# Output tiles copied from PSUM by ScalarE, the last one in halves, and transposes placed between output pieces in the last stretch

## Chip, cores and metric

One core of one Trainium2 chip. The metric is the device time of one execution in microseconds, the median of several runs. A trace is one profiled execution; times in it count from the start of its span, which is some 1.8 us shorter than the device time of that run (359.7 against 361.45). The experiments ran on several chips (8, 14, 11 and 12 in the record); a ratio compares runs of one occasion only, and the granted TensorE clock was 0.998 to 1.0 of full speed in every run for which it is listed.

## The reference

Two layers in a row. Clustered attention: each query and key is assigned to the nearest of 16 centroids of its head, and a query sees only keys of its own cluster. Then a gated feed-forward layer with RMS normalisation on the 3072 x 512 result.

```python
scores = where(q_assign == k_assign, q @ k.T / 8, -1e9)      # 4 batches, 8 heads, 768 x 64
x = softmax(scores) @ v                                      # becomes 3072 x 512
xn = x / sqrt(mean(x * x) + 1e-6) * rms_g
g = xn @ w_gate                                              # 512 x 1536
out = (g * sigmoid(g) * (xn @ w_val)) @ w_out                # 1536 x 512, float32
```

## The kernel before

The work is cut into eight units of 384 rows. While TensorE does the attention of unit u, the feed-forward products of units u-1 and u-2 are placed between its score products as filling. At a border between two stretches the normalised x of one unit is transposed, and the three output tiles of the unit before it are finished. Seven such borders exist: six lie beside attention, the last one has only feed-forward work around it.

TensorE's products go to tiles in PSUM, which the kernel takes in banks. All of `tq`, `tx`, gate, value and output products share three PSUM banks that rotate; a new tile waits until the one that had its bank has been read out (0.25 us listed for an output tile at 134.36 us, 0.77 us for the third transposes of the last border, both shown in the prediction).

```python
ps_s = pool("ps_s", 2, space=PSUM)      # scores, two banks each
ps_a = pool("ps_a", 1, space=PSUM)
ps_g = pool("ps_g", 3, space=PSUM)      # the three rotating banks
...
def rms(u):                             # sums of squares on ScalarE, the rest on VectorE
    ...
    for t in range(nt):
        squares(u, t, True)
    ...
def xtrans(u, c):
    ...
    ps = ps_g.tile([P, UQ], BF16, tag="gen", name="tx")
    ...
    for t in range(UNITS[u][2]):
        nc.tensor.transpose(ps[:, t * P:(t + 1) * P], xn[u][:, t, c * P:(c + 1) * P], ident)
    nc.vector.tensor_scalar_mul(xnT[u][:, c, :w], ps[:, :w], gcol[:, c:c + 1])
...
def out_mm(u, t, part):                 # an output tile, in three parts of four products
    ...
    if part == 0:
        outs[u] = ps_g.tile([P, DM], F32, tag="gen", name="o")
    for f in range(4 * part, 4 * part + 4):
        nc.tensor.matmul(outs[u], lhsT=gvT[u][:, f, t * P:(t + 1) * P], rhs=wo[:, f], start=f == 0, stop=f == FC - 1)
    if part == 2:
        o = outp.tile([P, DM], F32, tag="o_sb", name="o_sb")
        nc.vector.tensor_copy(o, outs[u])
        ...
        nc.sync.dma_start(out=rows[...], in_=o)
...
        # o: the nine output pieces of a border; ffn[:4]: its four transposes of x
        fill += o[:-3] + ffn[:2] + o[-3:-2] + ffn[2:3] + o[-2:-1] + ffn[3:4] + o[-1:] + spread(ffn[CC:CUT], prep)
        attention([(u, h) for h in range(H)], fill, 1)
...
rms(NU - 1)                             # the last border: outputs first, then the transposes
for _, f in out_work(NU - 2) + ffn_work(NU - 1) + out_work(NU - 1):
    f()
```

(Cuts are marked with dots; the comments are added here.)

The softmax here doesn't subtract the row's maximum and nothing guards it: scores larger than these inputs give would overflow.

## Time and profile before

| | before |
|---|---|
| time, median of 3 runs | 361.62 us (361.56 to 361.79) |
| span in the trace | 359.7 us |
| TensorE / ScalarE / VectorE busy | 96% / 71% / 66% |
| one output copy on VectorE, 128 x 512 | 0.69 us, 24 times |
| one table load on ScalarE (ACT_TABLE_LOAD) | 1.28 us, 3 times (at 2.63, 4.15 and 323.55 us) |
| TensorE's listed waits for output copies | 1.4 us, 5 times |

The first three rows say where to look: with TensorE at 96%, only its gaps can be won, and the last row lists those that belong to output copies. The lines themselves are in the prediction. In lines of the profile PE is TensorE (PEld its weight loads), DVE VectorE, ACT ScalarE, POOL GpSimd and SP SyncE; a q behind the name marks an instruction that only issues a transfer, and L379 is a line of that run's kernel. A timeline line gives the start, the duration, what ran and how often; the brackets hold the engine's idle time before it and what ended that. Lines of timelines are picked, those between are left out.

### The profile page before, as it was taken

Reading aid. Unit: us, or ns where it says so; the run is one execution under the profiler, and the core shown is the slowest. Engines: PE = TensorE matmul, PEld = TensorE weight load, DVE = VectorE, ACT = ScalarE, POOL = GpSimd, SP = SyncE. Lnnn points to the kernel's source line nnn. Section 1 sums busy time; section 2 is a strip of 40 time slices with the busy share of each in tenths; the row PEclk is TensorE's granted clock in tenths of the full one; section 3 lists DMA queues with packets and bytes.
Section 4 is the critical chain, followed back from the end, with each engine's and each line's share of the span. In section 5 each row is a group of like instructions: output and inputs, shape, how many; then the busy total and the mean of one; then the engine's idle time right before and its main releaser. Section 6 shows DMA issues by size and latency. Waiting matters only on the chain.

```text
span 359.7 us, 8049 instructions
## 1 busy us (share of the span) xinstructions
PE 345.2 (96%) x3027; PEld 210.0 (58%) x3047; DVE 237.1 (66%) x577; ACT 256.1 (71%) x455; POOL 110.2 (31%) x221
## 2 busy tenths in 40 slices
PE   8999799999999999999999999999999999999995
PEld 4555455655575656755576556756566656654552
DVE  5994379596567874686667865687656575677332
ACT  5789977996588866887588865978668866861320
POOL 1699306896051801535033711327000000000000
PEclk9999999999999999999999999999999999999999
DMA  7549999962154102610130002001010001002002
GB/s 256 185 121 212 244 241 270 334 190 67 64 157 133 24 29 89 202 40 19 59 118 2 16 8 87 2 2 24 38 52 3 0 31 58 2 3 80 8 2 87
DMA packets 28039, 32.03 MB, mean 89 GB/s; under 512 B 4960, under 2 KB 24928, under 8 KB 28000
## 3 DMA queue, kind: packets, MB, share of 16 engines
q1 hardware_dynamic: 18352, 24.75, 21.6%
q0 software_dynamic: 9072, 5.98, 10.0%
q10 hardware_dynamic: 576, 0.79, 0.7%
q8 instruction: 24, 0.39, 0.4%
q14 instruction: 15, 0.12, 0.1%
HBM read 28.35 MB, written 6.29 MB: 96 GB/s over the span
## 4 chain that ended last, share of the span: by engine, by line
PE 71%; DVE 14%; ACT 8%; issue 3%; POOL 1%; DMA 1%; SPq 0%; DVEq 0%; ACTq 0%
PE gate L357 16%; PE val L357 16%; PE s L284 13%; PE o L379 12%; PE acc L302 8%; ACT pT L288 5%; PE tq L200 4%; DVE o_sb L382 2%; PE sc L255 2%; ACT xn L322 2%; DVE xn L334 1%; PE warm L112 1%; DVE th L366 1%; DVE kext L214 1%; DVE scT L258 1%
## 5 line engine op out<-in xcount | busy, mean ns | idle before, releaser
L288 ACT ACTIVATE pT<-s,off 128x768 bf16<-128x768 f32 x192 | 171.0, 902 | 50.2 <-PE s L284 49.1
L284 PE MATMUL s<-qext,kext 80*128 80x384 bf16 x384 | 93.5, 325 | 3.0 <-ACT pT L288 2.6
L357 PE MATMUL gate<-xnT,wg 128*128 128x384 bf16 x384 | 78.5, 325 | 0.2 <-DVE xnT L345 0.2
L357 PE MATMUL val<-xnT,wv 128*128 128x384 bf16 x384 | 78.1, 326 | 0.4 <-DVE th L366 0.3
L366 DVE SCALAR_TENSOR_TENSOR th<-th,gate 128x384 f32<-128x384 f32 x84 | 46.3, 552 | 44.0 <-ACT th L365 43.6
L379 PE MATMUL o<-wo,gvT 128*128 128x512 bf16 x272 | 68.8, 378 | 2.1 <-DVE o_sb L382 1.0
L206 POOL CAST qext<-qkT 64x384 bf16<-64x384 f32 x64 | 33.0, 524 | 93.7 <-ACT qkT L202 92.1
L284 PEld LDWEIGHTS <-kext 80*128 80x128 bf16 x384 | 37.0, 98 | 35.3 <-issue 7.7
L365 ACT ACTIVATE th<-gate 128x384 f32<-128x384 f32 x84 | 41.1, 489 | 15.8 <-PE gate L357 15.2
L357 PEld LDWEIGHTS <-wv 128*128 128x128 bf16 x384 | 36.1, 97 | 26.1 <-issue 4.5
L370 DVE SCALAR_TENSOR_TENSOR gvT<-th,val 128x384 bf16<-128x384 f32 x84 | 46.1, 548 | 7.4 <-PE val L357 2.3
L357 PEld LDWEIGHTS <-wg 128*128 128x128 bf16 x384 | 35.8, 97 | 24.5 <-issue 3.6
L302 PEld LDWEIGHTS <-pT 128*128 128x128 bf16 x1152 | 43.5, 97 | 9.3 <-ACT pT L288 0.6
L302 PE MATMUL acc<-vbf,pT 128*128 128x65 bf16 x1152 | 45.6, 193 | 0.5 <-ACT pT L288 0.5
L379 PEld LDWEIGHTS <-gvT 128*128 128x128 bf16 x288 | 27.0, 97 | 27.7 <-issue 2.0
L202 ACT COPY qkT<-tq 128x384 f32<-128x384 f32 x64 | 29.2, 488 | 5.9 <-PE tq L200 5.0
L200 PE MATMUL tq<-ident_f,qk 128*128 128x128 f32 x192 | 30.2, 280 | 1.6 <-ACT qkT L202 1.2
L268 POOL DMA_DIRECT2D qext<-oh x48 | 23.1, 490 | 24.5 <-DVE oh L246 24.3
L200 PEld LDWEIGHTS tq<-ident_f,qk 128*128 128x128 f32 x192 | 23.2, 143 | 8.7 <-ACT qkT L202 2.2
L214 DVE TENSOR_SCALAR kext<-qkT 64x384 bf16<-64x384 f32 x60 | 23.8, 396 | 2.3 <-ACT qkT L202 1.6
L382 DVE COPY o_sb<-o 128x512 f32<-128x512 f32 x24 | 16.4, 686 | 12.5 <-PE o L379 12.5
L268 POOL DMA_DIRECT2D kext<-oh x48 | 22.9, 485 | 2.4 <-DVE th L366 1.2
(63 smaller groups left out, 241.9 us busy)
## 6 DMA issues: line engine op xcount, KB each, us to landing
qk<-in_q_dram SPq DMA_DIRECT2D x32, 192.0 KB, 3.9
vs<-in_v_dram SPq DMA_DIRECT2D x32, 192.0 KB, 3.7
out_dram<-o_sb SPq DMA_DIRECT2D x24, 256.0 KB, 2.0
qk<-in_k_dram SPq DMA_DIRECT2D x28, 192.0 KB, 4.0
wg<-in_moe_w_gate_dram POOLq DMA_DIRECT2D x4, 384.0 KB, 12.4
wv<-in_moe_w_val_dram POOLq DMA_DIRECT2D x4, 384.0 KB, 14.8
wo<-in_moe_w_out_dram POOLq DMA_DIRECT2D x3, 512.0 KB, 24.7
kext<-oh POOLq DMA_DIRECT2D x52, 12.0 KB, 1.6
```

The lines of the kernel that those rows point to most:

```text
L200: nc.tensor.transpose(ps[:, i * P:(i + 1) * P], qk[:, part, 2 * i:2 * i + 2].rearrange("p t d -> p (t d)"), ident_f)
L202: nc.scalar.copy(qkT[g, h // 2][:, h % 2, part], ps)
L206: nc.gpsimd.tensor_copy(qext[g % 4][:D, h, e * UQ:(e + 1) * UQ], qkT[g, h // 2][e * D:(e + 1) * D, h % 2, 0])
L268: on.dma_start(out=ext[D:D + NC, h, e * UQ:(e + 1) * UQ], in_=oh[32 * h + e * NC:32 * h + (e + 1) * NC])
L284: nc.tensor.matmul(ps[:, j, :w] if nt == HT else flat[:, j * w:(j + 1) * w], lhsT=kext[g % 4][:KR, hh, kc * P:(kc + 1) * P], rhs=qext[g % ...
L288: nc.scalar.activation(pT[u, h][:, n * i:n * i + n, :w], of, ACT.Exp, bias=off, scale=scale * ZS)
L302: nc.tensor.matmul(acc[:, h % 2, t], lhsT=pT[u, h][:, kc, t * P:(t + 1) * P], rhs=vbf[g % 4][:, hh, kc % HT * 2 + kc // HT], start=kc == 0 ...
L357: nc.tensor.matmul(ps, lhsT=w[:, c, f * P:(f + 1) * P], rhs=xnT[u][:, c, :n], start=c == 0, stop=c == CC - 1)
L365: nc.scalar.activation(th, ps, ACT.Tanh, scale=0.5)
L366: nc.vector.scalar_tensor_tensor(th, th, 1.0, ps, op0=ALU.add, op1=ALU.mult)
L370: nc.vector.scalar_tensor_tensor(gvT[u][:, f, :n], gates[u], 0.5, ps, op0=ALU.mult, op1=ALU.mult)
L379: nc.tensor.matmul(outs[u], lhsT=gvT[u][:, f, t * P:(t + 1) * P], rhs=wo[:, f], start=f == 0, stop=f == FC - 1)
```

## The change

Its intent: take the output copies from VectorE, which at a border is busy with the normalisation (131.14 to 132.42 us in the border shown below), to ScalarE, which idles there (1.22 us before the exponential at 133.87); fill the wait of the last border by mixing transposes and output pieces as in the other borders; halve the last copy, on which the end of the kernel hangs.

```diff
         if part == 2:
             o = outp.tile([P, DM], F32, tag="o_sb", name="o_sb")
-            nc.vector.tensor_copy(o, outs[u])
-            ...
-            nc.sync.dma_start(out=rows[...], in_=o)
+            ...                          # rows, now with the row index in it
+            if (u, t) == (NU - 1, HT - 1):
+                c = DM // 2
+                nc.vector.tensor_copy(o[:, :c], outs[u][:, :c])
+                nc.sync.dma_start(out=rows[:, :c], in_=o[:, :c])
+                nc.scalar.copy(o[:, c:], outs[u][:, c:])
+                nc.scalar.dma_start(out=rows[:, c:], in_=o[:, c:])
+            else:
+                nc.scalar.copy(o, outs[u])
+                nc.sync.dma_start(out=rows, in_=o)
...
+    def border(o, ffn):
+        return o[:-3] + ffn[:2] + o[-3:-2] + ffn[2:3] + o[-2:-1] + ffn[3:4] + o[-1:]
...
-    for _, f in out_work(NU - 2) + ffn_work(NU - 1) + out_work(NU - 1):
+    for _, f in border(out_work(NU - 2), ffn_work(NU - 1)) + ffn_work(NU - 1)[CC:] + out_work(NU - 1):
         f()
```

More of the change, by code (lines that the diff above doesn't have):

```diff
@@ L381, in out_mm @@
             o = outp.tile([P, DM], F32, tag="o_sb", name="o_sb")
-            nc.vector.tensor_copy(o, outs[u])
-            rows = out[b * S:(b + 1) * S].rearrange("(p t) f -> p t f", t=ST)
-            nc.sync.dma_start(out=rows[:, (col + t) % HT * 2 + (col + t) // HT], in_=o)
+            rows = out[b * S:(b + 1) * S].rearrange("(p t) f -> p t f", t=ST)[:, (col + t) % HT * 2 + (col + t) // HT]
+            if (u, t) == (NU - 1, HT - 1):
[7 more added lines that the diff above has]
+                nc.sync.dma_start(out=rows, in_=o)
     def group_work(g):
@@ L571 @@
         fill += [(0.0, lambda u=u: rms(u - 1))] + head
-        fill += o[:-3] + ffn[:2] + o[-3:-2] + ffn[2:3] + o[-2:-1] + ffn[3:4] + o[-1:] + spread(ffn[CC:CUT], prep)
+        fill += border(o, ffn) + spread(ffn[CC:CUT], prep)
         attention([(u, h) for h in range(H)], fill, 1)
```

## The prediction

> **What bounds the kernel now.** I read the busy shares first, then the slices, then who waits for whom on TensorE, and last the timeline around those waits.
>
> ```profile
> PE 345.2 (96%) x3027; PEld 210.0 (58%) x3047; DVE 237.1 (66%) x577; ACT 256.1 (71%) x455; POOL 110.2 (31%) x221
> PE   8999799999999999999999999999999999999995
> PEclk9999999999999999999999999999999999999999
> ```
>
> TensorE is busy for 96% of the span at the full granted clock. The slices with room are the first five and the last one; between them nothing but a TensorE gap can be won. So the question is which TensorE gaps the change touches. The waits of TensorE name two that concern the output tile o_sb (columns: us in total, times, longest):
>
> ```profile
> PE o L379 <- DVE o_sb L382: 1.0, 4, 0.3
> PE tx L344 <- DVE o_sb L382: 0.4, 1, 0.4
> ```
>
> The four waits are one in each of four borders between stretches (about 88, 130, 172 and 213 us). One border, in order of time (start, us, engine, what):
>
> ```profile
> 131.14 1.28 DVE L334 TENSOR_SCALAR xn<-x,ny 128x512 bf16<-128x512 f32 x3
> 131.56 1.89 PE L379 MATMUL o<-wo,gvT 128*128 128x512 bf16 x8
> 131.75 0.90 ACT L288 ACTIVATE pT<-s,off 128x768 bf16<-128x768 f32 x1 [0.84 <-PE s L284]
> 132.33 0.68 DVE L382 COPY o_sb<-o 128x512 f32<-128x512 f32 x1
> 132.93 0.19 DVE L307 RECIPROCAL inv<-acc 128x6 f32<-128x6 f32 x1
> 133.15 0.56 DVE L309 TENSOR_TENSOR x<-acc,inv 128x384 f32<-128x384 f32 x1
> 133.28 0.49 PE L284 MATMUL s<-qext,kext 80*128 80x384 bf16 x2
> 133.61 0.50 PE L344 MATMUL tx<-ident,xn 128*128 128x128 bf16 x6
> 133.63 0.68 DVE L382 COPY o_sb<-o 128x512 f32<-128x512 f32 x1
> 133.87 0.90 ACT L288 ACTIVATE pT<-s,off 128x768 bf16<-128x768 f32 x1 [1.22 <-PE s L284]
> 134.36 1.02 PE L379 MATMUL o<-wo,gvT 128*128 128x512 bf16 x3 [0.25 <-DVE o_sb L382]
> ```
>
> The reader should see a queue on VectorE. It works in order: normalisation of x until 132.42, the copy of output tile 0, the reciprocal and scaling of attention, and only then the copy of tile 1, which TensorE had finished at 133.28. Three PSUM banks rotate, and in the compiled program output tile 2 takes the bank of tile 1, so TensorE stands until 134.36. Meanwhile ScalarE is idle for 1.22 us.
>
> The wait of 0.25 us understates the stall. Elsewhere three transposes push the next output matmul back by 0.17 us (137.45 to 137.62), so six from 133.61 would let it start at 133.95. It starts at 134.36: a stall of 0.41 us.
>
> The last border and the end are in the chain that ended last:
>
> ```profile
> 323.09 7.51 PE o L379 x34
> 330.60 0.02 issue
> 330.63 0.70 DVE o_sb L382
> 331.33 0.04 issue
> 331.37 0.65 PE tx L344 x6
> 332.02 0.65 PE gate L357 x3
> ...
> 355.82 0.02 issue
> 355.84 0.69 DVE o_sb L382
> ```
>
> Here all three output tiles run back to back and the transposes follow; the third transpose group needs the bank of tile 2 and waits 0.77 us for its copy (330.60 to 331.37). The final copy takes 0.69 us, and 3.17 us of store and closing follow it to 359.7.
>
> [...] in the compiled changed kernel ScalarE's half copy waits for the same VectorE count as the store of VectorE's half does. The two halves are one after the other.
>
> [...] the load at 4.15 us is followed by an activation at 5.44. I use 1.28 us.
>
> [...]
>
> **The change part by part.** Durations first. The copy leaves VectorE at 688 ns. ScalarE has never copied 512 columns here; its PSUM copies of 384 columns take 488 ns, and 128 more [...] make 595 ns. For 256 columns that gives 381 ns on ScalarE, and 688 less 256 at 1.04 ns (the slope between VectorE's PSUM copy of 128 columns, 288 ns, and this one), 421 ns on VectorE. These three are estimates.
>
> *Load moved.* VectorE loses 23.5 copies, 16.2 us, and falls from 66% to about 61%. ScalarE gains 23 of 0.595 and a half of 0.381, about 14 us, and goes from 71% to 75%. Neither is the bound, so this itself is worth nothing.
>
> *Four borders.* In the compiled order the copy of tile 1 stands on ScalarE between the exponential that starts at 131.75 (over at 132.65) and the one at 133.87. It would start at 133.30 and end at 133.90; with 0.04 us of hand-over TensorE may go at 133.94, when its transposes are done anyway. The stall of 0.41 is gone: 4 x 0.41 = 1.64 us. The following exponential is due at 133.87 and starts there or a few hundredths later; TensorE needs it a microsecond later.
>
> *The two later borders (about 259 and 296 us).* There VectorE is free when tile 1 ends and its copy starts at once, at 259.00, so only the shorter copy counts: 0.09 each, 0.2 us.
>
> *Last border.* New order: tiles 0 and 1, transposes 0 and 1, then output pieces and transposes in turn. Tile 1 ends at 322.81 + 24 x 0.2164 = 328.00, after x is normalised (327.67), so the transposes can start. Tile 2 needs the bank of tile 1: copy 328.02 to 328.62, start 328.66, though the two transposes are through at 328.34, so 0.32 us of new stall. Twelve output matmuls (2.60) and two transpose groups (0.34) end at 331.60, and the first gate starts there, since its bank depends on a transpose and not on tile 2. Before it began at 332.02, stood 0.32 us for the last transposed piece and lost 0.09 at the third gate, effectively 332.43.
>
> But the table load for Silu now stands behind the copy of tile 2. In the kernel before it ran at 323.55, unseen. Now: copy to 332.22, load to 333.52, first Silu to 334.02, hand-over 334.06. The second value group takes that Silu's bank and would be due at 331.60 + 3 x 0.65 = 333.55, so it stands 0.51 us. Effective start 332.11, a gain of 0.32 us.
>
> *End.* 0.02 + 0.42 + 0.04 + 0.38 = 0.86 us in place of 0.71 until the last half is in SBUF: 0.15 lost. The last store is half as large: 12 KB land in 1.6 us and 256 KB in 2.0, so 128 KB save about 0.2. I take 0 for the end.
>
> Sum: 1.64 + 0.2 + 0.32 = 2.2 us, which would give 359.4. I hold back some 0.2 us for delays of exponentials and tanh behind the copies of tiles 0 and 2, and predict 359.6.
>
> **The rivals.** *ScalarE becomes the engine waited for.* Its copies wait in line for TensorE, and exponentials stand behind them. For it: TensorE already waited 2.6 us in 8 places for exponentials. Against: nearly all of that is before 84 us, where no output is copied, and in each border ScalarE idles about a microsecond before each exponential. If it held, 0.3 us per border in six borders would cancel the gain: about 361.3.
>
> *The won time is given back at the next wait.* TensorE arriving 0.41 us earlier could meet a late transposed x, q or k. For it: chains through VectorE are tight after each border. Against: the copies leave VectorE, so its work there also comes earlier by about 0.7 us. If half is given back: about 360.5.
>
> *The table load is hoisted [...].* Without any cost from it the time would be about 359.1[...].
>
> **Range and chances.** The middle part is the surest, since the idle engine and the stall are both seen; full success with a cheaper end gives 358.9[...]. I take 358.8 to 361.0. All readings lie within 2% (354.4 to 368.9), since only about 4 us of TensorE idling lie in the part that the change reaches: faster 0.01, same 0.98, slower 0.01.
>
> **What would show it.** Right: no wait of the output matmuls on o_sb in the four borders, each stretch about 0.4 us shorter, copies of near 595 ns on ScalarE, the table load after the third copy of the last border with a TensorE gap of about 0.5 us at the second value group, and the two half copies one after the other. Wrong: new waits of the score matmuls on exponentials, output matmuls waiting for ScalarE's copy by as much as before, or a span that shrinks less than its borders do. The prediction fails above 361.0 if ScalarE's order costs more than its idle time hides, and below 358.8 if the end gains from two stores.

## The result

The changed kernel took 360.01 us, median of 4 runs (359.34 to 360.25), beside 361.59 (360.60 to 361.79) for the kernel before. The ratio is 0.9959, with a 95% interval of 0.9936 to 0.9981; repeated on another occasion with 5 runs it was 360.12 us and 0.9965 (0.9953 to 0.9978). A ratio is the mean time of one kernel's fast runs over that of the other's fast runs of the same rounds, so it is not quite the ratio of the medians. By the 2% rule every kernel of this document that was timed more than once counts as the same.

Runs differ by a microsecond, as much as the effect, so I read the traces by stretches. The marks are start times of the same instructions in each trace: the fourth exponential of the third stretch (before the first output copy), the first exponential of the seventh stretch, the last exponential, the third value group of the last stretch, the last matmul, the end of the span. Times in us:

| trace | up to the first mark | four borders | two borders | last border | filling | end | from the first mark on |
|---|---|---|---|---|---|---|---|
| before | 81.58 | 161.71 | 72.69 | 19.54 | 19.91 | 4.24 | 278.08 |
| changed | 80.82 | 160.74 | 72.49 | 19.55 | 19.91 | 4.05 | 276.74 |
| changed, second trace | 81.62 | 160.73 | 72.48 | 19.55 | 19.90 | 4.05 | 276.72 |

From the first mark on the two traces of the changed kernel agree to 0.02 us, and it is 1.35 us faster than before: 0.97 in four borders (0.24 each), 0.20 in two (0.1 each), nothing in the last border, 0.19 at the end. The first column is another matter. Up to there the programs are the same, and yet it went from 80.82 to 82.19 us over the 14 traces of this study. That is where the spread of the traced runs comes from, and part of it is there at the first exponential already (15.37 to 16.11 us); why, I did not find out. The first trace of the changed kernel had 0.76 us of luck there.

The changed page, busy shares and the group of the new copies (busy us, mean ns of one, idle before):

```profile
PE 345.1 (97%) x3047; PEld 209.3 (59%) x3047; DVE 222.8 (62%) x554; ACT 267.8 (75%) x479; POOL 110.7 (31%) x221
L390 ACT COPY o_sb<-o 128x512 f32<-128x512 f32 x23 | 13.5, 586 | 19.1 <-PE o L379 18.6
```

TensorE has hardly moved from 345.2 us: it does the same work in a shorter span. The copy takes 586 ns on ScalarE, where 595 was estimated. That estimate and the 381 ns for a half (372 measured) rest on a time per column that no copy in the trace before had shown; from its squares of x, 524 ns for 384 columns and 303 for 128, 0.86 ns a column, they would be about 598 and 378. TensorE's waits now, of those that concern the argument:

```profile
PE s L284 <- ACT pT L288: 2.6, 8, 0.8
PE val L357 <- ACT th L363: 0.5, 1, 0.5
PE o L379 <- ACT o_sb L390: 0.3, 1, 0.3
```

The first line, 2.6 us in 8 places, was in the kernel before too, to the tenth: in no wait of the list does ScalarE's fuller queue hold up a score product. The waits for o_sb in the four borders are gone from the list. They are not quite gone from the chip, as the border at 131 us shows:

```profile
131.33 0.19 DVE L307 RECIPROCAL inv<-acc 128x6 f32<-128x6 f32 x1
132.27 0.49 PE L284 MATMUL s<-qext,kext 80*128 80x384 bf16 x2
132.47 0.59 ACT L390 COPY o_sb<-o 128x512 f32<-128x512 f32 x1 [0.83 <-PE o L379]
132.60 0.50 PE L344 MATMUL tx<-ident,xn 128*128 128x128 bf16 x6
133.11 1.02 PE L379 MATMUL o<-wo,gvT 128*128 128x512 bf16 x4
```

Compare with the same border in the prediction. VectorE goes straight from the normalisation to the reciprocal, and ScalarE copies tile 1 from 132.47. But the six transposes start at 132.60 and tile 2 at 133.11, 0.51 us later, where six transposes take 0.34. ScalarE's copy ended at 133.06. So 0.17 of the former 0.41 us is still a wait for the copy; no list shows it, since the profile counts TensorE as busy until the modelled end of the last transpose (132.60 + 0.50).

The last border (the cut leaves out the alternating pieces):

```profile
325.91 0.50 PE L344 MATMUL tx<-ident,xn 128*128 128x128 bf16 x6
326.11 0.59 ACT L390 COPY o_sb<-o 128x512 f32<-128x512 f32 x1 [2.00 <-PE o L379]
326.75 1.02 PE L379 MATMUL o<-wo,gvT 128*128 128x512 bf16 x4 [0.34 <-ACT o_sb L390]
...
329.67 0.81 PE L357 MATMUL gate<-xnT,wg 128*128 128x384 bf16 x4
329.87 0.59 ACT L390 COPY o_sb<-o 128x512 f32<-128x512 f32 x1 [3.17 <-PE o L379]
330.47 1.28 ACT L363 ACT_TABLE_LOAD   x1
331.76 0.87 ACT L363 ACTIVATE th<-gate 128x384 f32<-128x384 f32 x2
332.31 0.81 PE L357 MATMUL val<-xnT,wv 128*128 128x384 bf16 x4 [0.53 <-ACT th L363]
```

Tile 2 starts 0.84 us after the transposes, behind the copy of tile 1. Then the table load of 1.28 us stands between the copy of tile 2 and the first Silu, and the second value group, due 0.65 us after 330.97, starts at 332.31: a stall of 0.69 us.

The end:

```profile
353.92 0.42 DVE L385 COPY o_sb<-o 128x256 f32<-128x256 f32 x1 [7.14 <-DMA out_dram<-o_sb]
354.38 0.37 ACT L387 COPY o_sb<-o 128x256 f32<-128x256 f32 x1 [2.46 <-DVE o_sb L385]
354.79 0.35 ACTq L388 DMA_DIRECT2D out_dram<-o_sb  x1
```

ScalarE's half starts at 354.38, 0.03 us after VectorE's half has ended (353.92 + 0.42): one after the other, as the wait in the compiled program asked; whether the chip itself needs that wait, no run here tried. The note on VectorE's idle time before its half names a DMA; that is the page's choice of the latest of several waits, and the last output matmul ended at 353.89, just before the copy began. The last half landed at 356.53, 1.74 us after its issue. In the kernel before the whole tile took 2.01.

### The profile page after: what moved, and what is told of

The parts are those of the page before. It is cut to its first block, busy times and chain, and to the rows that moved or that the text cites. A ratio compares the mean times of both kernels' runs of the same rounds, so it can differ in the third digit from the quotient of the medians.

```text
span 357.6 us, 8075 instructions
## 1 busy us (share of the span) xinstructions
PE 345.1 (97%) x3047; PEld 209.3 (59%) x3047; DVE 222.8 (62%) x554; ACT 267.8 (75%) x479; POOL 110.7 (31%) x221
## 4 chain that ended last, share of the span: by engine, by line
PE 81%; ACT 7%; DVE 5%; issue 2%; DMA 2%; POOL 1%; ACTq 1%; SPq 0%; DVEq 0%
PE o L379 17%; PE val L357 16%; PE gate L357 16%; PE s L284 15%; PE acc L302 9%; PE tq L200 4%; ACT pT L288 4%; PE sc L255 3%; PE tx L344 1%; ACT xn L322 1%; DMA vs<-in_v_dram 1%; DVE kext L214 1%; PE warm L112 1%; DVE th L366 1%; POOL kext L494 1%
## 5 line engine op out<-in xcount | busy, mean ns | idle before, releaser
L379 PE MATMUL o<-wo,gvT 128*128 128x512 bf16 x288 | 70.5, 378 | 0.4 <-ACT o_sb L390 0.3
L390 ACT COPY o_sb<-o 128x512 f32<-128x512 f32 x23 | 13.5, 586 | 19.1 <-PE o L379 18.6
L345 DVE TENSOR_SCALAR xnT<-tx,gcol 128x384 bf16<-128x384 bf16 x32 | 12.7, 415 | 23.4 <-PE tx L344 23.2
```

## The experiments

Each is compared by stretches from the first mark on, as above, since the time up to there is chance. Seven kernels (the order alone, the halves alone, tile 1 alone, the whole last copy, the two stores, the split last tile, the other bank) were run once, for their trace: a single run does not tell its state, so their times are not compared. Their stretches can be: those that an edit does not touch repeat to 0.02 us. All results were correct.

**Copies alone** (on the kernel before)

```diff
-            nc.vector.tensor_copy(o, outs[u])
+            nc.scalar.copy(o, outs[u])
```

> The kernel before with nothing changed but the copy's engine: all 24 output copies on ScalarE, whole, order of the last border and last store as before. Theory 'parts': the gain of the change comes from the borders in the middle (0.24 us in each of four, 0.11 in each of two, 1.2 in all), so this kernel gains 1.2 there, about 0.1 at the last border (the shorter copy before the third transposes) and 0.1 at the end (0.59 for 0.69 us), 1.4 in all, as much as the whole change. Rival 'last stretch': the reordering and the halves carry the gain, and this kernel gains under 0.8 us in the trace after the first copy.

Measured: four borders 160.73, two 72.48, last border 19.30, end 4.13; 276.54 from the first mark on, which is 1.54 us less than before and 0.2 less than the whole change. Timed: 359.67 us (4 runs), ratio 0.9952 (0.9937 to 0.9967). So moving the engine of the copy is the whole gain, and the other two parts of the change take away a little in sum. The last border gained 0.24, not 0.1: beside the shorter copy VectorE, no longer copying, scales the transposed x sooner (its first one starts 0.37 us after the first transposes, where before it was 0.80).

**The order of the last border alone** (on the kernel before)

```diff
-    for _, f in out_work(NU - 2) + ffn_work(NU - 1) + out_work(NU - 1):
+    o, ffn = out_work(NU - 2), ffn_work(NU - 1)
+    for _, f in o[:-3] + ffn[:2] + o[-3:-2] + ffn[2:3] + o[-2:-1] + ffn[3:4] + o[-1:] + ffn[CC:] + out_work(NU - 1):
```

> The kernel before with only the order of the last border changed; copies stay on VectorE. Nothing may change before the last border. Theory 'table load': without a copy on ScalarE the Silu table is loaded early and unseen, so the second value group doesn't stand for it; but VectorE copies tile 1 only after normalising x, so tile 2 starts near a microsecond after the transposes. Worked out: third value group 0.2 us earlier against the border's start than in the kernel before, and earlier than in the changed kernel, which gained 0.0. Rival 'order is harmful': 0.2 us or more later than before.

Measured: last border 19.20 for 19.54, so 0.34 us earlier, more than expected; the middle unchanged (161.72 and 72.69). Tile 2 starts 1.08 us after the first transposes, because VectorE copies late, as expected; but the table load ran at 323.03, unseen. The order is good by itself. In the changed kernel its gain is eaten, and the next experiment shows by what.

**Halves alone** (on the kernel before: the last tile as in the change, all other copies on VectorE)

```diff
+            if (u, t) == (NU - 1, HT - 1):
+                ...                          # the two half copies and stores of the change
+            else:
+                nc.vector.tensor_copy(o, outs[u])
+                nc.sync.dma_start(out=rows, in_=o)
```

> The kernel before with only the last tile copied in halves by two engines and stored in two. Both theories: from the last output matmul to the end of the span 0.2 us shorter than 4.24 us, with the copies ending 0.14 us later and the store of a half landing 0.27 us faster; the two copies one after the other, not side by side. Rival: if the halves overlap, the copies end 0.25 us earlier than before.

Measured: end 4.04 for 4.24, everything else as before. VectorE's half ended at 356.01 and ScalarE's started at 356.04.

**Early table load** (on the changed kernel)

```diff
             squares(u, t, True)
+        if u == NU - 1:
+            nc.scalar.activation(first_exp, off, ACT.Silu)
```

> The changed kernel with one more Silu on a single column just after the last sums of squares, so that the table load comes before the three copies. Theory 'table load behind the copy': the stall of 0.69 us at the second value group (330.97 to 332.31 for one group of 0.65) vanishes, and the kernel is 0.6 to 0.7 us faster from the last border on. Rival: the stall comes from the bank's hand-over and stays, or the load delays the copy of tile 0 and the time comes back at tile 2.

Measured: last border 18.87 for 19.55, 0.68 us; all else as in the changed kernel; 359.11 us, ratio 0.9931 (0.9914 to 0.9947). The wait of the value group is gone from the list. The load now runs while TensorE works through the 5.2 us of output products that start at 321.46:

```profile
322.35 1.28 ACT L329 ACT_TABLE_LOAD   x1
323.64 0.20 ACT L329 ACTIVATE first_exp<-off 128x1 f32<-128x1 f32 x1
324.24 0.59 ACT L392 COPY o_sb<-o 128x512 f32<-128x512 f32 x1 [0.40 <-PE o L381]
```

The copy of tile 0 follows at 324.24, when its matmuls are done, with 0.4 us of idle time before it. This settles the last border: the load behind the copy cost 0.68 us and hid what the new order had won.

**Tile 1 alone** (on the kernel before)

```diff
-            nc.vector.tensor_copy(o, outs[u])
+            if t == 1 and u < NU - 2:
+                nc.scalar.copy(o, outs[u])
+            else:
+                nc.vector.tensor_copy(o, outs[u])
```

> The kernel before with one output copy in three on ScalarE: that of tile 1 of each border but the last stretch's own; tiles 0 and 2 stay on VectorE. Theory 'bank of tile 1': the middle's gain is the earlier end of this one copy, so tile 2 starts 0.24 us earlier in each of the four borders and 0.11 in the two later ones, 1.2 us in all, as with all copies moved. Rival 'VectorE relieved': the gain comes from 16 us less work on VectorE, and a third of the copies gives a third of it, 0.4 us.

Measured: four borders 160.73, two 72.48, the same as with all copies moved; last border 19.55 and end 4.25 as before. Six copies out of 24 make the whole gain of the middle. In one border:

```profile
131.64 0.68 DVE L385 COPY o_sb<-o 128x512 f32<-128x512 f32 x1
132.78 0.58 ACT L383 COPY o_sb<-o 128x512 f32<-128x512 f32 x1 [0.83 <-PE o L379]
133.42 1.02 PE L379 MATMUL o<-wo,gvT 128*128 128x512 bf16 x4
```

VectorE still copies tile 0 after its normalisation; ScalarE takes tile 1, and tile 2 follows 0.05 us after that copy has ended. VectorE's 16 us of relief are worth nothing in the middle.

**Whole last copy** (on the changed kernel)

```diff
-                c = DM // 2
-                ...                          # two half copies, two half stores
+                nc.scalar.copy(o, outs[u])
+                nc.sync.dma_start(out=rows, in_=o)
```

> The changed kernel with its last tile copied whole by ScalarE and stored once. From the last output matmul's start to the end 4.05 us in the changed kernel. Theory: the copy ends 0.24 us earlier (0.59 for 0.43 and 0.37 in a row) and the store lands 0.27 later (2.01 for 1.74), so 4.05 to 4.15, the halves being worth nothing over a whole copy by the faster engine. Rival: the second engine helps, and this is 0.2 us or more slower.

Measured: end 4.12 for 4.05. So the halves are worth 0.07 us over a whole copy by ScalarE.

**Whole copy, two stores** (on the changed kernel)

```diff
-                nc.vector.tensor_copy(o[:, :c], outs[u][:, :c])
+                nc.scalar.copy(o, outs[u])
                 nc.sync.dma_start(out=rows[:, :c], in_=o[:, :c])
-                nc.scalar.copy(o[:, c:], outs[u][:, c:])
                 nc.scalar.dma_start(out=rows[:, c:], in_=o[:, c:])
```

> As the run before it, but the whole copy is stored in two halves from two queues at once. If a store's time goes with the bytes in flight together, both land about 2.0 us after issue and nothing is won over one store; if a half lands in 1.74 whatever else is in flight, the end comes 0.25 us earlier, about 3.8 us after the last output matmul's start.

Measured: end 4.21, 0.09 us worse than one store. Issued together, the halves landed after 1.86 and 2.08 us. In the runs whose two halves were issued 0.41 us or more apart, both landed in 1.69 to 1.74 us.

**Split last tile** (on the changed kernel)

```diff
+        ...                              # rows, moved up here
+        if (u, t) == (NU - 1, HT - 1):
+            if part < 2:
+                c = slice(part * DM // 2, (part + 1) * DM // 2)
+                half = ps_g.tile([P, DM // 2], F32, tag="gen", name="oh")
+                for f in range(FC):
+                    nc.tensor.matmul(half, lhsT=gvT[u][:, f, t * P:(t + 1) * P], rhs=wo[:, f, c], start=f == 0, stop=f == FC - 1)
+                o = outp.tile([P, DM], F32, tag="o_sb", name="o_sb")[:, :DM // 2]
+                nc.scalar.copy(o, half)
+                nc.sync.dma_start(out=rows[:, c], in_=o)
+            return
```

> The changed kernel with the last output tile computed as two column halves in two banks, each copied by ScalarE and stored when it is done, so that the first half's copy and store lie beside the second half's matmuls. From the end of the last matmul only one half copy (0.37) and one half store (1.74) remain: about 0.45 us less than in the changed kernel after the last matmul. The 24 half-width matmuls at an estimated 0.109 us apart (128, 384 and 512 columns stand 0.057, 0.163 and 0.216 apart) take 2.62 for 2.60 us; if loading the weights twice binds instead, TensorE ends later and eats the gain.

Measured: filling 20.04 and end 3.49, together 23.53 for 23.96 in the changed kernel, 0.43 us less. The 24 products took 2.62 us, where 12 of full width take 2.59: loading the weights twice cost 0.03 us. The tail as it stands in the next kernel but one, which has the same split:

```profile
351.45 0.37 ACT L386 COPY o_sb<-oh 128x256 f32<-128x256 f32 x1 [0.72 <-PE oh L384]
351.85 1.69 SPq L387 DMA_DIRECT2D out_dram<-o_sb  x2
352.80 0.37 ACT L386 COPY o_sb<-oh 128x256 f32<-128x256 f32 x1 [0.98 <-PE oh L384]
```

The first half's copy ends at 351.82 and its store is issued at 351.85, while TensorE still works on the second half, whose copy starts at 352.80. The two engines on one bank had not given that overlap: their copies followed each other at 0.03 us.

**Another bank for tile 2 of the last border** (on the kernel with the early load)

```diff
-            outs[u] = ps_g.tile([P, DM], F32, tag="gen", name="o")
+            if (u, t) == (NU - 2, HT - 1):
+                outs[u] = ps_s.tile([P, 2, 512], F32, tag="s", name="s")[:, 0]
+            else:
+                outs[u] = ps_g.tile([P, DM], F32, tag="gen", name="o")
```

> The changed kernel with the early Silu load and, in the last border, tile 2 in one of the score banks, which nobody uses by then. Theory: of the last border's costs 0.5 us are the wait of tile 2 for the bank of tile 1 (0.84 us from the first transpose to tile 2, of which six transposes are 0.34), so it starts 0.5 us earlier and the third value group 1.2 us earlier than in the changed kernel, counted from the border's start. Rival: another wait, for the transposed x or the third transpose's bank, takes its place, and less than 0.2 us comes on top of the early load.

Measured: last border 18.36 for 18.87, 0.51 us less, and 1.19 less than in the changed kernel. The score banks lie idle after the last exponential, so the wait could be removed without a faster copy.

**All that helped** (early load, other bank, split last tile)

> All that should help together: early Silu load, tile 2 of the last border in a score bank, the last tile in two column halves. If the parts add up: 0.7 and 0.5 us from the last border and up to 0.45 from the end, 1.5 us faster than the changed kernel and near 3 us faster than before, ratio to before 0.992 or a little less.

Measured: 275.09 from the first mark on, 1.65 us less than the changed kernel; 358.49 us, median of 5, ratio 0.9921 (0.9907 to 0.9934). The parts (0.68, 0.51, 0.43) add up to 1.62.

**The changed kernel again**

> The changed kernel again on the same chip, for a second trace and more rounds. What lies before the first output copy (77 us) is the same program as before: if its 0.5 us of difference between the first two traces is chance, it differs by some tenths here too, in either direction; from there on the parts should repeat: 0.24 us in each of four borders, 0.11 in two, 0.0 in the last, 0.2 at the end. The ratio should lie at 0.996.

Measured: the row in the table of the result. The first mark came at 81.62, near the 81.58 of the kernel before: the 0.76 us of the first trace was chance.

**Tile 2 later in the middle borders** (on the kernel with all that helped; the scheduler places filling by cost, so cost is moved from one piece to another)

```diff
-        return o[:-3] + ffn[:2] + o[-3:-2] + ffn[2:3] + o[-2:-1] + ffn[3:4] + o[-1:]
+        if not o:
+            return ffn[:4]
+        shift = 0.7
+        wide, slim = (ffn[1][0] + shift, ffn[1][1]), (o[-3][0] - shift, o[-3][1])
+        return o[:-3] + ffn[:1] + [wide, slim] + ffn[2:3] + o[-2:-1] + ffn[3:4] + o[-1:]
```

> The kernel with all that helped, and in the borders in the middle the first piece of output tile 2 put behind the next score and attention products instead of before them. Theory 'the copy starts late': a matmul's results are complete some 0.2 us after its successor starts, so in the changed kernel ScalarE's copy of tile 1 still ends 0.17 us after the transposes, hidden in no listed wait; with other products in between, this rest goes in four borders: 0.17 each, 0.7 us less than the kernel without this move, counted from 81 us on. Rival: the six transposes take 0.51 us by themselves after scores and nothing waits: then nothing changes.

Measured: four borders 160.05 for 160.73, 0.68 us less; 274.42 from the first mark on. 358.07 us, median of 6 (357.93 to 359.19), ratio 0.9911 (0.9890 to 0.9931). One border:

```profile
133.67 0.59 ACT L402 COPY o_sb<-o 128x512 f32<-128x512 f32 x1 [0.83 <-PE o L395]
133.80 0.50 PE L346 MATMUL tx<-ident,xn 128*128 128x128 bf16 x6
134.13 0.49 PE L284 MATMUL s<-qext,kext 80*128 80x384 bf16 x2
135.01 1.03 PE L395 MATMUL o<-wo,gvT 128*128 128x512 bf16 x3
```

The six transposes start at 133.80 and the score products 0.33 us later: so long are six transposes, and the 0.51 of the changed kernel was a wait. The copy ends at 134.26, behind other products. This is the fastest version, 3.2 us below the 361.28 of the kernel before in the same rounds.

## Why the prediction was right, and where it was not

The time, 359.6 predicted and 360.0 measured, fell within the range, and nothing suggests more than 2%. The range was wide for an effect of this size: 358.8 to 361.0 is a gain of 0.6 to 2.8 us. The sum of the parts was 2.2 us; from the first mark on the change brought 1.35: 0.67 too little in four borders and 0.32 too little in the last, 0.19 more at the end. Nor does its upper end follow from the parts: on top of 359.6, half of the middle given back (0.92) makes 360.5, and the 0.5 us from there to 361.0 was an estimate that no trace showed.

*What bounds the kernel, and ScalarE as rival.* Right. TensorE's gaps decided; ScalarE went to 75% as said and the waits for exponentials stayed at 2.6 us in 8 places.

*Four borders: the mechanism right, one term wrong.* The stall of 0.41 us in the kernel before was real: with tile 1's copy out of the way (the last experiment) the rest of it goes too. But the step "It would start at 133.30" failed. I took the start of the next score product (133.28) as the end of tile 1. ScalarE's copy started 0.20 us after that product's start (132.47 after 132.27), so it ended later than the transposes, and 0.24 of 0.41 us went, four times: 0.97 for 1.64. VectorE's copy had started 0.56 us after the start of tile 1's last matmul, in each of the four borders; ScalarE's starts 0.42 after it. So passing by VectorE's queue is worth 0.15 of the 0.24, and the shorter copy (0.59 for 0.68) the other 0.09. The information was in the lines I showed: output matmuls stand 0.216 us apart but their records last 0.378, so a matmul's end lies 0.16 us after the next one's start. The end of a record is modelled; what the trace measured is the copy's start, 0.20 us after the next product's. I had not carried it into the hand-over.

*Two later borders.* 0.09 each predicted, 0.1 measured: there both engines' copies start 0.42 us after the last matmul's start, and only the length of the copy counted.

*Last border.* 0.32 predicted, nothing measured. The gate's start came out as predicted (2.35 us earlier than before where the stretch began 1.93 earlier, so 0.42), but by luck, since two errors cancelled. The sum let tile 0 begin at 322.81, where the chain's piece begins; its first matmul had started at 322.66. And tile 2 stood 0.50 us behind the transposes (0.84 less their 0.34) and not 0.32, again by the late start of a copy. Right was the table load as the thing that eats the gain. Two more terms were off, and these did not cancel. The table's stall was 0.69 and not 0.51, from the same late start of a copy: 329.87, 0.20 after the gate's start, where my sum leaves 0.02. And the old border's own loss was counted 0.16 too high: "stood 0.32 us" took the chain's piece for the fourth gate matmul, 0.32, as stall, though half of it is the length of that matmul; value groups start 0.65 us apart and the first stood 0.81 after its gate.

*End.* 0 predicted, 0.19 measured. The copies ended 0.14 later, as estimated (0.15), and a half store landed 0.27 faster where I put 0.2; the rest, 0.06, is the closing after the last landing, 1.03 for 1.09 us. (After the old kernel's last copy 3.14 us follow, 356.53 to 359.67, not 3.17.)

*Rivals.* The table load was not hoisted: it ran from 330.47, right after the copy of tile 2 (over at 330.46), for 1.28 us, and the first Silu starts at 331.76, 0.01 us after its end. Nothing of the middle's gain was given back: 0.24 in the border shown is 0.97 in four, and in all nine kernels that copy tile 1 with ScalarE and keep the order of the middle, the four borders take 160.73 to 160.75 us.

## What to carry to other kernels

When a bank changes hands between TensorE and a copying engine, count from the end of the last matmul's record and not from the start of the next product (here the copy began 0.20 us after that start), and look for waits that hide under a modelled tail: the distance between starts tells them (here 0.51 us where six transposes take 0.34). Before moving work to an engine with a table to load, see where the load goes (here 1.28 us, behind which TensorE stood 0.69); a single small activation ahead of the moved work put it where nobody waits (0.68 us won). And ask which copy somebody waits for: here 6 of 24 made the gain of the middle, and in the last border a free bank (0.51 us) did more than the faster engine (0.24).
